# Decay attention and a two-layer MLP on one core: the first batch's decay made on GpSimd, its rows turned in float32, the weights converted by block

## The chip, the cores and the metric

The kernel runs on one core of one Trainium2 chip. The metric is device time in microseconds (us) for one execution. The engines are TensorE (PE, with its weight loads shown apart as PEld), VectorE (DVE), ScalarE (ACT), GpSimd (POOL) and SyncE (SP), which here only issues transfers. Each engine runs its own instructions in the order in which they stand. Transfers are issued on SP's queue, on POOL's queue and, for the output, on ACT's queue, and run on 16 DMA engines.

## The reference, cut to what matters

```python
# q, k, v: 8 batches x 8 heads x 576 rows x 64;  f: 8 x 8 x 576
scores = q @ k.T / sqrt(64)
cum    = cumsum(log(clip(f, 1e-4, 1)))            # per head, along the rows
scores = where(causal, -1e9, scores + cum[:, None] - cum[None, :])
attn   = exp(scores - max) / (sum + 1e-9)
x      = concat over heads (attn @ v)             # 4608 tokens x 512
h      = x @ w_in                                 # w_in 512 x 2048, stored as float64
g      = where(h >= 1, h, where(h <= -1, 0, (h + 1)**2 / 4))
out    = g @ w_out                                # w_out 2048 x 512, stored as float64
```

## The kernel before, in words

**Attention** is cut into 36 jobs, each one pair of heads of one batch. The first batch is cut once more along the query rows (`CUTS`): jobs 0 to 3 are its four pairs with rows 0 to 255, jobs 4 to 7 the same pairs with rows 256 to 575; from job 8 on, four jobs make a batch. A job goes by blocks of 128 query rows (r = 0 to 4, the last with 64 rows and both heads in one tile).

A job's steps are: q and k are loaded (`load`, line 400) and turned (`prepare`; jobs below `NQK` = 12 keep them in float32, later ones split them in two float16 parts and turn these by a DMA transpose, `qkT<-qs`). `scores` multiplies them (line 511). The decay, cum of the row minus cum of the column, enters in one of two ways. For jobs below `NDEC` = 8, that is the whole first batch, six bfloat16 rows per head (`w.dec`, loaded from `dec_d` at line 416 into a buffer of the ring `vm`) are multiplied into the same PSUM tile, and the causal mask comes from the constant tiles `hide`. From job 8 on, a row of cum is broadcast to 128 partitions (`ck`, line 411, POOL's queue) and POOL makes decay (line 521) and mask (line 525) in an SBUF tile `sdr` or `sd`. `weights` then adds score and decay on DVE and takes the row minimum of the negated sum (line 604), ACT does the exponential (line 608). For jobs below `NPE` = 5 `turn_rows` multiplies the weights by a diagonal matrix on PE in float32, which scales and transposes them at once (lines 545 and 551), ACT copies them to `pT` (line 556), and `early_values` multiplies by v in float32 (line 576). From job 5 on the rows are split into two float16 parts (ACT line 622, DVE line 628, or POOL line 626 for some of jobs 6 and 7), turned by DMA transposes (`pT<-pr`, lines 634 and 637), and multiplied by v in three float16 passes (`values`, line 648). The result goes to `x` (ACT line 583 or 657, DVE line 584 or 658).

**Scales.** From batch 1 on `value_scale` takes the largest |v| of a batch, and from batch 2 on `query_scale` the largest |q| and |k|. Each reads its arrays in tiles of 288 KB on POOL's queue (lines 282 and 306) into `vm`, a ring of two buffers, and takes a maximum on DVE (lines 283 and 307). A load waits until a buffer of `vm` is free. `across` makes a maximum common to all partitions: a transpose on PE (line 125), four small DVE operations, a product on PE (line 135) between them, and `scale_of` three more on DVE.

**Weights.** They come as 32 pieces of 512 KB (float64). Each is packed to float32 by three DVE operations (lines 232, 235, 238), then scaled into a high and a low float16 part: ACT line 259; POOL lines 261 and 262 for w_in, DVE line 264 for w_out. `weight_split` handles half a block (two pieces): the bound for the scale is a maximum on DVE for w_in (line 248) and a sum of |w| on ACT for w_out (line 252), then one `across` per half block, 16 in all. `CONVERT` and `LOADS` tell in which job; `RAW` tells where a raw piece waits.

**The MLP** goes by units: 256 tokens times one of 8 blocks of d_ff, 144 units. `moe_front` (line 690) and `moe_back` (line 718) are PE's, with ACT and DVE between them (lines 699 to 704). A unit can run when its tokens are in `x` and its block is converted; `quota` spreads the ready units over the jobs. `EARLY` lets units of the first 256 tokens begin with the blocks that are converted.

The program is written in this order, and a scheduler then sets the order on each engine and each queue ahead of the run.

Of the kernel before, what the change touches and what calls it, by code (L numbers as in the profile page):

```python
# [10 lines left out]
BF16 = mybir.dt.bfloat16  # L11
# [5 lines left out]
P = 128  # L17
# [12 lines left out]
NPE = 5  # L30

NQK = 12
NDEC = 8

POOL_LOW = {6: (2, 4), 7: (2, 4)}
# [3 lines left out]
CONVERT = {3: 3, 4: 3, 5: 4, 6: 4, 7: 2}  # L39
LOADS = {0: 2, 1: 3, 2: 4}  # L40
AHEAD = 4

RAW = (
    (1, 2), (3, 4), (5, 6), (7, 8), (9, 10), (11, 12), (16, 17), (18, 19),
    (20, 13), (14, 15), (11, 12), (16, 17), (18, 19), (20, 14), (15, 16), (17, 18),
# [4 lines left out]
def kernel(  # L50
# [10 lines left out]


# [80 lines left out]
    NR = 6  # L143
    NDH = NDEC // (2 * NPAIR) * H
    dec_d = dram.tile([NDH, NR, 2, S], BF16, name="dec_d")
# [3 lines left out]
    def decay_sums():  # L149

# [3 lines left out]
        rows = one.tile([P, NT5, 2, 2, S], F16, name="pT").rearrange("p t l h s -> p (t l h s)").bitcast(BF16)  # L154
        rows = rows[0:NDH, 0:NR * 2 * S].rearrange("p (r j s) -> p r j s", r=NR, j=2)
        nc.gpsimd.memset(fl[0:nb, 3 * S:4 * S], 0.0)
        nc.gpsimd.memset(rows[:, 1::2, 0], 1.0)
        nc.gpsimd.memset(rows[:, 0::2, 1], 1.0)
# [3 lines left out]
        nc.scalar.activation(fl[0:nb, S:2 * S], fl[0:nb, 0:S], AF.Ln)  # L162
        cum = fl[0:nb, 2 * S:3 * S]
# [3 lines left out]
        rest = fl[0:NDH, 0:S]  # L167
        nc.vector.tensor_scalar(out=rest, in0=cum[0:NDH], scalar1=8.0, scalar2=None, op0=ALU.mult)
        for i in range(3):
            part = rows[:, 2 * i, 0]  # L170
            nc.scalar.activation(part, rest, AF.Copy)
            nc.scalar.activation(rows[:, 2 * i + 1, 1], part, AF.Copy, scale=-1.0)
            if i < 2:
                nc.vector.tensor_tensor(out=rest, in0=rest, in1=part, op=ALU.subtract)
# [3 lines left out]
        twice = fl[0:nb, S:S + P]  # L178
# [12 lines left out]
    hides = one.tile([P, 2, 2, SP], F16, name="qs").rearrange("p j l e -> p (j l e)").bitcast(F32)  # L191
    hide, hide4 = hides[:, 0:FULL], hides[:, FULL:FULL + S]
    for t, h in ((hide, 1), (hide4, 2)):
        n = P // h
        wide = t.shape[1]
        nc.gpsimd.memset(t, 0.0)
        for i in range(h):
            a = t[n * i:n * i + n, wide - n:wide]
            nc.gpsimd.affine_select(
                a, a, pattern=[[-1, n]], channel_multiplier=1, base=0, compare_op=ALU.is_ge, fill=MASKED  # L200
            )


# [9 lines left out]
    def weight_load(n):  # L213
        i, j = divmod(n, 2)
        if j == 0:
            src = w_in.bitcast(I32)[:, i * 4 * P:(i + 1) * 4 * P].rearrange("(t p) c -> p t c", p=P)
        else:
            src = w_out.bitcast(I32)[i * 2 * P:(i + 1) * 2 * P, :].rearrange("(t p) c -> p t c", p=P)
        n = src.shape[1] // 2
        for k_, slot in enumerate(RAW[2 * i + j]):  # L220
            nc.sync.dma_start(
                slots[slot].rearrange("p (t c) -> p t c", t=n), src[:, n * k_:n * (k_ + 1), :]
            )

    def weight_split(n):
        i, j = divmod(n, 2)
        parts = []
        for k_, slot in enumerate(RAW[n]):
# [12 lines left out]
            parts.append((top.bitcast(F32), slice(k_ * DM, (k_ + 1) * DM)))  # L241
        hi = place[n][:, 0]
        lo = place[n][:, 1]
        m1 = tiny.tile([P, 1], F32, name="m1", bufs=2)
        ms = tiny.tile([P, 2], F32, name="ms", bufs=2)
        for k_, (wf, c) in enumerate(parts):
            if j == 0:
                nc.vector.tensor_reduce(
                    out=ms[:, k_:k_ + 1], in_=wf, axis=AX.X, op=ALU.max, apply_absolute_value=True
                )  # L250
# [7 lines left out]
        for wf, c in parts:  # L258
            nc.scalar.activation(hi[:, c], wf, AF.Copy, scale=s)
            if n % 2 == 0:  # L260
                nc.gpsimd.tensor_scalar(out=wf, in0=wf, scalar1=s, scalar2=0.0, op0=ALU.mult, op1=ALU.add)
                nc.gpsimd.tensor_tensor(out=lo[:, c], in0=wf, in1=hi[:, c], op=ALU.subtract)
            else:
                nc.vector.scalar_tensor_tensor(
                    out=lo[:, c], in0=wf, scalar=s, in1=hi[:, c], op0=ALU.mult, op1=ALU.subtract
                )
# [219 lines left out]
    def scores(w, r):  # L486
# [28 lines left out]
        if w.p < NDEC:  # L515
            return
# [360 lines left out]
```

## Time and profile before

| | |
|---|---|
| time, median of 3 runs | 1243.08 us (1237.45 to 1243.55) |
| the profiled execution | 1248.13 us; its span, first to last instruction, 1246.4 us |
| PE busy | 1071.5 us, 86% of the span |
| DVE, ACT, POOL busy | 830.1 us, 765.8 us, 438.7 us |
| mean granted TensorE clock | 0.930 |
| DMA | 163.27 MB, mean 131 GB/s |

Busy shares are means over the whole span. The profile also gives the span in 40 slices, tables of the engines' busy time in any stretch, and rows of single instructions with the idle time before them and what ended it. The table's "PEclk" is the clock that was granted to TensorE as a share of full speed.

### The profile page before, as it was taken

The numbers are of one execution on the slowest core, as the hardware profiler recorded it, in microseconds if no ns is written. First come the engines' busy times: TensorE is split into PE (matmuls) and PEld (weight loads), VectorE is DVE, ScalarE is ACT, GpSimd is POOL, SyncE is SP. The second block draws the span as 40 slices with busy tenths as digits, with TensorE's granted clock in tenths as the row PEclk, the third lists the DMA queues.
The fourth block names the chain that finished last, engine by engine and source line by source line (L and its number), as shares of the span: only waits on it lengthen the run. The fifth ranks groups of instructions, "written<-read, shape, count | busy, mean of one in ns | idle before, by whom it ended". The sixth has DMA issues, their size and how long they took to land. (4 is left out here: it accounts for less than half of the span.)

```text
span 1246.4 us, 24524 instructions
## 1 busy us (share of the span) xinstructions
PE 1071.5 (86%) x8859; PEld 675.2 (54%) x8859; DVE 830.1 (67%) x2227; ACT 765.8 (61%) x1564; POOL 438.7 (35%) x752
## 2 busy tenths in 40 slices
PE   1569646798327988999999999999999999999998
PEld 1336333454215654665666666656566566667665
DVE  5747879788658777877765576687766877622222
ACT  2456545466436586777766676686777777734443
POOL 2021244464455463544532323454534444100000
PEclk9868767699667998999999999999999999999999
DMA  8822564598999888886756656577777675500000
GB/s 235 277 51 63 143 151 147 143 205 205 180 206 210 179 171 155 163 162 137 147 104 110 127 111 114 120 141 151 141 135 141 128 130 90 93 17 3 18 18 17
DMA packets 404906, 163.27 MB, mean 131 GB/s; under 512 B 384840, under 2 KB 384840, under 8 KB 404776
## 3 DMA queue, kind: packets, MB, share of 16 engines
q1 hardware_dynamic: 389040, 113.33, 48.6%
q0 software_dynamic: 10560, 38.94, 11.6%
q10 hardware_dynamic: 5184, 9.44, 2.1%
q8 instruction: 69, 1.13, 0.4%
q14 instruction: 53, 0.43, 0.1%
HBM read 86.61 MB, written 9.70 MB: 77 GB/s over the span
## 5 line engine op out<-in xcount | busy, mean ns | idle before, releaser
L690 PE MATMUL ph<-x,place 128*128 128x256 f16 (+3 forms) x4608 | 436.1, 249 | 36.9 <-DVE u L701 23.9
L718 PE MATMUL po<-place,g 128*128 128x512 f16 x1728 | 415.9, 383 | 7.1 <-ACT g L703 4.8
L690 PEld LDWEIGHTS <-place 128*128 128x128 f16 x4608 | 355.2, 99 | 115.7 <-issue 41.1
L718 PEld LDWEIGHTS <-g 128*128 128x128 f16 x1728 | 162.3, 99 | 181.3 <-issue 9.5
L521 POOL TENSOR_SCALAR sdr<-ck,nsig,cqs 128x128 f32<-128x128 f32 (+1 forms) x192 | 156.7, 820 | 290.4 <-DVE pr L628 278.0
L608 ACT ACTIVATE sdr<-sdr,nm 128x384 f32<-128x384 f32 (+1 forms) x248 | 137.8, 557 | 117.4 <-DVE nm L604 116.7
L701 DVE SCALAR_TENSOR_TENSOR u<-ph,z,u 128x512 f32<-128x512 f32 x136 | 101.5, 747 | 106.2 <-ACT u L700 105.8
L699 ACT ACTIVATE u<-ph,z 128x512 f32<-128x512 f32 x136 | 104.5, 768 | 76.3 <-PE ph L690 75.4
L628 DVE SCALAR_TENSOR_TENSOR pr<-sdr,rc,pr 128x384 f16<-128x384 f32 (+2 forms) x232 | 122.0, 561 | 38.9 <-ACT pr L622 36.2
L703 ACT ACTIVATE g<-u,z 128x512 f16<-128x512 f32 x136 | 97.7, 719 | 74.0 <-DVE u L701 73.5
L622 ACT ACTIVATE pr<-sdr,rc 128x384 f16<-128x384 f32 (+1 forms) x236 | 119.8, 556 | 34.2 <-ACT sdr L608 14.1
L704 DVE SCALAR_TENSOR_TENSOR g<-u,z,g 128x512 f16<-128x512 f32 x136 | 104.2, 766 | 47.6 <-ACT g L703 47.4
L648 PE MATMUL big<-pT,vs 128*64 128x64 f16 (+3 forms) x1098 | 94.7, 300 | 34.7 <-DMA pT<-pr 33.2
L604 DVE CUSTOM_DVE_ANT_0 sdr<-s,sdr,nalpha 128x128 f32<-128x128 f32 (+1 forms) x192 | 98.5, 546 | 21.3 <-PE s L511 13.1
L511 PE MATMUL s<-qkT 64*128 64x128 f16 (+5 forms) x704 | 91.7, 356 | 20.2 <-DVE nm L604 16.0
L648 PEld LDWEIGHTS <-vs 128*64 128x64 f16 x1098 | 61.5, 117 | 74.5 <-issue 45.6
L700 ACT ACTIVATE u<-u 128x512 f32<-128x512 f32 x144 | 89.7, 624 | 2.4
L525 POOL TENSOR_SCALAR_AFFINE_SELECT sdr<-sdr 128x128 f32<-128x128 f32 x224 | 77.4, 352 | 7.7
L521 POOL TENSOR_SCALAR sd<-ck,nsig,cqs 64x576 f32<-64x576 f32 x48 | 46.1, 960 | 78.2 <-DMA ck<-cum_d 65.5
L511 PEld LDWEIGHTS <-qkT 64*128 64x128 f16 (+1 forms) x864 | 33.2, 99 | 58.2 <-issue 44.6
L433 DVE SCALAR_TENSOR_TENSOR qs<-qk,sqk,qs 128x640 f16<-128x640 f32 x48 | 42.3, 907 | 27.3 <-ACT qs L432 26.9
L432 ACT ACTIVATE qs<-qk,sqk 128x640 f16<-128x640 f32 x48 | 37.1, 819 | 36.2 <-DMA qkT<-qs 30.3
(174 smaller groups left out, 1077.8 us busy)
## 6 DMA issues: line engine op xcount, KB each, us to landing
ck<-cum_d POOLq DMA_DIRECT2D x56, 288.0 KB, 4.7
out_dram<-ot ACTq DMA_DIRECT2D x36, 256.0 KB
qk<-in_k_dram SPq DMA_DIRECT2D x64, 128.0 KB
vm<-in_v_dram POOLq DMA_DIRECT2D x28, 288.0 KB, 3.9
v<-in_v_dram SPq DMA_DIRECT2D x62, 128.0 KB
qk<-in_q_dram SPq DMA_DIRECT2D x56, 128.0 KB
vm<-in_q_dram POOLq DMA_DIRECT2D x24, 288.0 KB, 3.5
vm<-in_k_dram POOLq DMA_DIRECT2D x24, 288.0 KB, 3.8
```

The source lines that it names most:

```text
L511: nc.tensor.matmul(outs[h][:, c0:c1], lhsT=x[rows], rhs=y[rows, c0:c1], start=(i == 0), stop=(i == len(terms) - 1),)
L521: nc.gpsimd.tensor_scalar(out=sd[p0:p1, 0:wid], in0=w.ck[h][p0:p1, 0:wid], scalar1=w.nsig if w.p < NQK else w.nsig[p0:p1], scalar2=w.cqs[p ...
L604: nc.vector.tensor_tensor_reduce(out=a, in0=sp, in1=other, scale=w.nalpha, scalar=BIG, op0=ALU.add, op1=ALU.min, accum_out=nm[:, i:i + 1],)
L608: nc.scalar.activation(a, a, AF.Exp, bias=nm[:, i:i + 1], scale=-1.0, accum_out=sm[:, i:i + 1])
L622: nc.scalar.activation(pr[:, :, 0, i, :], a, AF.Copy, scale=rc[:, i:i + 1])
L628: nc.vector.scalar_tensor_tensor(out=pr[:, :, 1, i, :], in0=a, scalar=rc[:, i:i + 1], in1=pr[:, :, 0, i, :], op0=ALU.mult, op1=ALU.subtract,)
L648: nc.tensor.matmul(av[64 * h:64 * h + 64, at + s0:at + s1], lhsT=w.vs[:, vl, h, t, :], rhs=w.pT[:, t, pl, h, s0:s1], start=(t == 0 and pi ...
L690: nc.tensor.matmul(ph[:, fi, a0:a1], lhsT=wi[fb][:, wl, t, fi * P:(fi + 1) * P], rhs=xs[b][:, t, xl, s0:s0 + a1 - a0], start=(fi == 0 and ...
L699: nc.scalar.activation(u, h, AF.Relu, scale=z.u[:, i:i + 1], bias=z.h[:, i:i + 1])
L701: nc.vector.scalar_tensor_tensor(out=u, in0=h, scalar=z.t[:, i:i + 1], in1=u, op0=ALU.max, op1=ALU.min)
L704: nc.vector.scalar_tensor_tensor(out=g[:, 1], in0=u, scalar=z.r[:, i:i + 1], in1=g[:, 0], op0=ALU.mult, op1=ALU.subtract)
L718: nc.tensor.matmul(po[ch][i], lhsT=g[:, gl, fi * TC + i * P:fi * TC + (i + 1) * P], rhs=wo[fb][:, wl, fi, :], start=(first and fi == 0 and ...
```

## The change

- **Decay.** `NDEC` and all that belongs to it go: the six bfloat16 rows, `dec_d`, their loads on SP, the product of six rows, the `hide` tiles. Jobs 0 to 7 take the way of the later jobs: `ck`, and decay and mask on POOL. For jobs below 12 the load of `ck` moves from POOL's queue to SP's, and only the columns in use are loaded. The ring `vm` no longer holds decay rows.
- **Weights.** `weight_split` handles a whole block, four pieces; both bounds are sums of |w| on ACT, and one `across` takes two columns: 8 in place of 16. `CONVERT`, `LOADS`, `AHEAD` and `RAW` are new: conversion runs from job 1 to job 6 (before, 3 to 7).
- **Rows of the first batch.** `NPE` goes from 5 to 8: jobs 5, 6 and 7 use `turn_rows` and `early_values`. `POOL_LOW` goes.

```diff
-NPE = 5
+NPE = 8
...
-NDEC = 8
-
-POOL_LOW = {6: (2, 4), 7: (2, 4)}
...
-CONVERT = {3: 3, 4: 3, 5: 4, 6: 4, 7: 2}
-LOADS = {0: 2, 1: 3, 2: 4}
-AHEAD = 4
+CONVERT = {1: 1, 2: 1, 3: 1, 4: 2, 5: 2, 6: 1}
+LOADS = {0: 2, 1: 3}
+AHEAD = 3
...
-        nc.sync.dma_start(dec_d, rows)
         nc.sync.dma_start(cum_d, cum)
...
-        for k_, (wf, c) in enumerate(parts):
-            if j == 0:
-                nc.vector.tensor_reduce(
-                    out=ms[:, k_:k_ + 1], in_=wf, axis=AX.X, op=ALU.max, apply_absolute_value=True
-                )
+            if k_ < 0:
+                nc.vector.tensor_reduce(out=m, in_=wf, axis=AX.X, op=ALU.max, apply_absolute_value=True)
             else:
-                nc.scalar.activation(lo[:, c], wf, AF.Abs, accum_out=ms[:, k_:k_ + 1])
+                nc.scalar.activation(low.bitcast(F32), wf, AF.Abs, accum_out=m)
+        m1 = tiny.tile([P, 2], F32, name="m1w", bufs=2)
         nc.vector.tensor_reduce(out=m1, in_=ms, axis=AX.X, op=ALU.max)
-        m = mi[:, i:i + 1] if j == 0 else tiny.tile([P, 1], F32, name="m2")
+        m = tiny.tile([P, 2], F32, name="m2", bufs=2)
         across(m, m1)
-        s = sw[:, j, i:i + 1]
-        scale_of(s, mp[:, j, i:i + 1], m)
+        nc.vector.tensor_copy(mi[:, i:i + 1], m[:, 0:1])
+        scale_of(sw[:, :, i], mp[:, :, i], m)
...
-        if w.p >= NDEC:
-            ck = two.tile([P, S], F32, name="ck", bufs=3)
-            nc.gpsimd.dma_start(ck, cum_d[bh:bh + 1].broadcast_to([P, S]))
-            w.ck.append(ck)
-            return
-        if h == 0:
-            w.dec = two.tile([P, S], F32, name="vm").bitcast(BF16).rearrange("p (j s) -> p j s", j=2)
-        nc.sync.dma_start(w.dec[64 * h:64 * h + NR], dec_d[bh])
+        ck = two.tile([P, S], F32, name="ck", bufs=3)
+        (nc.sync if w.p < NQK else nc.gpsimd).dma_start(ck[:, 0:w.s1], cum_d[bh:bh + 1, 0:w.s1].broadcast_to([P, w.s1]))
+        w.ck.append(ck)
...
-        if w.p < NDEC:
-            terms.append((w.dec[:, 0, s0 + w.s0:s1 + w.s0], w.dec[:, 1], NR))
...
-        if w.p < NDEC:
-            return
...
-            other = a if w.p >= NDEC else hide[:, FULL - wid:FULL] if r < LAST else hide4
```

What moves in the order of the instructions stands in three places. In the changed kernel line numbers are smaller: 185 for 221, 372 for 411 and 416, 244 and 268 for 282 and 306, 245 and 269 for 283 and 307, 474 and 478 for 521 and 525, 556 for 604.

SP's queue near the start, before: `place` and `in_moe` are weight pieces, `vm<-dec_d` the decay rows of jobs 0 and 1.

```order
L221 DMA place_108<-in_moe_w_in_dram 128x2x512
L221 DMA place_109<-in_moe_w_in_dram 128x2x512
L400 DMA qk_0_132<-in_q_dram 128x2x64 x2
L404 DMA qk_0_132<-in_q_dram 64x2x64
L404 DMA qk_0_132<-in_k_dram 64x2x64
L221 DMA place_110<-in_moe_w_out_dram 128x1024
L221 DMA place_111<-in_moe_w_out_dram 128x1024
L404 DMA qk_1_133<-in_q_dram 64x2x64
L404 DMA qk_1_133<-in_k_dram 64x2x64
L416 DMA vm<-dec_d 6x1152 x4
```

The same queue now:

```order
L362 DMA qk_0_119<-in_q_dram 128x2x64 x2
L362 DMA qk_0_119<-in_k_dram 128x2x64 x2
L185 DMA place_100<-in_moe_w_in_dram 128x2x512
L372 DMA ck<-cum_d 128x256 x3
L185 DMA place_101<-in_moe_w_in_dram 128x2x512
L185 DMA place_102<-in_moe_w_out_dram 128x1024
```

The first job's decay stands behind one weight piece, where eight stood ahead of it.

POOL's queue near the start, now (before, three loads of `ck` and the low parts of the weights stand here, and no line 521 or 525 until job 8):

```order
L244 DMA vm<-in_v_dram 128x576 x2
L268 DMA vm<-in_q_dram 128x576
L474 TENSOR_SCALAR sdr_122<-ck,cq_89 128x128
L474 TENSOR_SCALAR sdr_124<-ck,cq_89 128x256
L474 TENSOR_SCALAR sdr_123<-ck,cq_89 128x128
L478 AFFINE_SELECT sdr_122<-sdr_122 128x128
L474 TENSOR_SCALAR sdr_125<-ck,cq_89 128x256
L474 TENSOR_SCALAR pr_132<-ck,cq_89 128x128
L474 TENSOR_SCALAR pr_134<-ck,cq_89 128x256
L268 DMA vm<-in_q_dram 128x576
L478 AFFINE_SELECT sdr_124<-sdr_124 128x128
```

Loads of later batches' q, k and v now stand among the decay of the first jobs; each waits on POOL for a buffer of `vm`.

DVE in job 9, before:

```order
L307 TENSOR_REDUCE m_5298<-vm 128x1
L115 RECIPROCAL sqk<-mk 128x2
L316 TENSOR_SCALAR nsig<-sqk 128x1
L319 RECIPROCAL nalpha<-nsig 128x1
L320 TENSOR_SCALAR cqs_129<-cq_90,nsig 128x40
L433 SCALAR_TENSOR_TENSOR qs<-qk_0_132,sqk,qs 128x640 x2
L604 ISA sdr_135,nm<-s,sdr_135 128x384
```

DVE in job 6, now, among the packing of weight pieces:

```order
L228 SCALAR_TENSOR_TENSOR place_103<-place_104,sw,place_103 128x512
L269 TENSOR_REDUCE m_5265<-vm 128x1 x3
L196 TENSOR_SCALAR u<-place_106 128x512
L269 TENSOR_REDUCE m_5265<-vm 128x1
L199 SCALAR_TENSOR_TENSOR u<-place_106,u 128x512
L648 SCALAR_TENSOR_TENSOR u<-ph,early_z,u 128x512
L202 SCALAR_TENSOR_TENSOR place_106<-place_106,u 128x512
```

The same maxima stand three jobs earlier. Counted over DVE's order: ahead of job 7's write to `x` stand 21 of them before and 56 now, ahead of job 11's 65 and 68. On PE, ahead of job 7's product with v stand the fronts of 8.4 units before and 6.0 now, ahead of job 11's 16.9 and 16.5, and ahead of job 35's 113.6 and 114.8.

More of the change, by code (lines that the diff above doesn't have):

```diff
@@ L10 @@
 F16 = mybir.dt.float16
-BF16 = mybir.dt.bfloat16
 I32 = mybir.dt.int32
@@ L166, in decay_sums @@
         )
[L167 to L174, printed above, removed]
-        nc.sync.dma_start(dec_d, rows)
         nc.sync.dma_start(cum_d, cum)
         pt = ps1.tile([P, 1024], F32, name="big")
-        twice = fl[0:nb, S:S + P]
+        twice = fl[0:nb, 0:P]
         nc.vector.tensor_copy(
@@ L240, in weight_split @@
             )
[L241 to L245, printed above, removed]
-        for k_, (wf, c) in enumerate(parts):
-            if j == 0:
-                nc.vector.tensor_reduce(
-                    out=ms[:, k_:k_ + 1], in_=wf, axis=AX.X, op=ALU.max, apply_absolute_value=True
-                )
-            else:
-                nc.scalar.activation(lo[:, c], wf, AF.Abs, accum_out=ms[:, k_:k_ + 1])
+            wf = top.bitcast(F32)
@@ L255, in weight_split @@
         across(m, m1)
-        s = sw[:, j, i:i + 1]
-        scale_of(s, mp[:, j, i:i + 1], m)
-        for wf, c in parts:
-            nc.scalar.activation(hi[:, c], wf, AF.Copy, scale=s)
-            if n % 2 == 0:
+        nc.vector.tensor_copy(mi[:, i:i + 1], m[:, 0:1])
+        scale_of(sw[:, :, i], mp[:, :, i], m)
+        for k_, wf in enumerate(wfs):
+            j = k_ // 2
+            s = sw[:, j, i:i + 1]
+            c = slice(k_ % 2 * DM, (k_ % 2 + 1) * DM)
+            hi, lo = place[2 * i + j][:, 0, c], place[2 * i + j][:, 1, c]
+            nc.scalar.activation(hi, wf, AF.Copy, scale=s)
+            if k_ < 2:
@@ L763, in load_weights @@
         nonlocal nload
-        while nload < min(n, 2 * NB) and not any(set(RAW[nload]) & set(r) for r in RAW[nw:nload]):
+        while nload < min(n, NB) and not any(set(RAW[nload]) & set(r) for r in RAW[nw:nload]):
             weight_load(nload)
@@ L837 @@
             while ready() and done - before < quota * (i + 1) // len(steps):
-                if units[done] not in bsc and nw < 2 * NB:
+                if units[done] not in bsc and nw < NB:
                     break
```

79 lines of the change are left out of this document (29 added, 50 removed).

## The prediction

> **What bounds the kernel now.** I read the page's shares and slices first, then the table of engines by stretch, then the rows that bound the stretches.
>
> ```profile
> PE 1071.5 (86%) x8859; PEld 675.2 (54%) x8859; DVE 830.1 (67%) x2227; ACT 765.8 (61%) x1564; POOL 438.7 (35%) x752
> ...
> PE   1569646798327988999999999999999999999998
> ...
> PEclk9868767699667998999999999999999999999999
> DMA  8822564598999888886756656577777675500000
> ```
>
> The mean of 86% hides two halves: from slice 13 on PE is full, ahead of it are holes, a lower granted clock and, in slices 9 to 13, full DMA engines. The ends of the stretches come from ACT's rows that write `x`: job 7 (last of batch 0) and job 11 (last of batch 1).
>
> ```profile
> 238.44 0.44 ACT L657 ACTIVATE x<-big 128x320 f16<-128x320 f32 x1 [8.90 <-PE big L648]
> ...
> 380.00 0.65 ACT L657 ACTIVATE x<-big 128x576 f16<-128x576 f32 x1 [1.65 <-PE big L648]
> ```
>
> ```profile
> core 0: us, PE busy (x) PEld busy (x) DVE busy (x) ACT busy (x) POOL busy (x), PEclk, DMA share, GB/s
> 0.00:238.00 238.00, 145.22 (x767) 85.48 (x767) 170.02 (x504) 115.96 (x254) 64.75 (x96) 0.77 0.56 153
> 238.00:380.00 142.00, 91.87 (x627) 52.45 (x629) 104.25 (x301) 73.56 (x167) 70.67 (x131) 0.83 0.90 193
> 380.00:600.00 220.00, 200.12 (x1904) 129.20 (x1902) 171.14 (x473) 157.81 (x332) 111.68 (x191) 0.96 0.86 165
> 600.00:1246.00 646.00, 634.27 (x5565) 408.08 (x5564) 384.65 (x951) 418.46 (x813) 191.63 (x335) 1.00 0.51 97
> ```
>
> After 600 us PE is busy 634 of 646 us, and by the counts in the part on the change as many units are left after job 11 as before (16.9 fronts done, then 16.5). So the end moves with job 11's end, less what the stretch 380 to 600 (20 us of PE idle) gives or takes; I set that at zero. The sum has two parts: **stretch one**, 0 to 238, and **stretch two**, 238 to 380.
>
> **Stretch two.** Its fullest resource is DMA: 0.90 of 142 is 128 us.
>
> ```profile
> q1 hardware_dynamic: 47152, 11.70, 49.4%
> q0 software_dynamic: 3940, 14.54, 37.8%
> ...
> vm<-in_k_dram POOLq DMA_DIRECT2D x16, 288.0 KB, 4.0
> vm<-in_q_dram POOLq DMA_DIRECT2D x13, 288.0 KB, 3.4
> vm<-in_v_dram POOLq DMA_DIRECT2D x13, 288.0 KB, 4.0
> ck<-cum_d POOLq DMA_DIRECT2D x8, 288.0 KB, 5.1
> ```
>
> POOL's queue q0 carried 50 loads in 37.8% of 142, 53.7 us, so 1.07 us of all 16 engines for each. Of the maxima for which `vm` is loaded, 44 stand between job 7's and job 11's writes (21 to 65); now 12 (56 to 68). The ring is free from the start, since decay rows no longer sit in it, and the scheduler has drawn the loads into batch 0. DMA loses 32 x 1.07 = 34 us and comes to 94. DVE loses the maxima:
>
> ```profile
> L307 DVE TENSOR_REDUCE m<-vm 128x1 f32<-128x576 f32 x48 | 35.7, 747 | 23.4 <-DMA vm<-in_k_dram 12.7 <-DMA vm<-in_q_dram 10.0
> ...
> L248 DVE TENSOR_REDUCE ms<-place 128x1 f32<-128x512 f32 x12 | 8.0, 677 | 0.1
> ...
> L127 DVE TENSOR_REDUCE top<-s 1x1 f32<-1x128 f32 x24 | 6.5, 273 | 5.3 <-PE s L125 5.2
> ...
> L136 DVE COPY m<-s 128x1 f32<-128x1 f32 x8 | 1.2, 154 | 7.2 <-PE s L135 7.2
> ```
>
> 32 x 0.747 = 24 us, so 104 becomes 80. PE gets more: 10.5 fronts stand in the stretch (6.0 to 16.5) where 8.5 stood (8.4 to 16.9).
>
> ```profile
> L690 PE MATMUL ph<-x,place 128*128 128x256 f16 (+3 forms) x4608 | 436.1, 249 | 36.9 <-DVE u L701 23.9
> L718 PE MATMUL po<-place,g 128*128 128x512 f16 x1728 | 415.9, 383 | 7.1 <-ACT g L703 4.8
> ```
>
> A unit is (436.1 + 415.9) / 144 = 5.9 us, two are 12 (14 at this stretch's clock of 0.83), so PE comes to 104 and is now the fullest. Before, the fullest filled 0.90 of the stretch; PE at the same share needs 104 / 0.90 = 115 us. **Gain 26 us**, between 0 (the jobs' own chains set the pace, whatever the DMA does) and 38 (PE full).
>
> That chains and DMA, not PE, set the pace there shows in its last two jobs, and what chains alone do in jobs 3 and 4:
>
> ```profile
> 52.00:79.00 27.00, 19.52 (x100) 12.16 (x98) 9.50 (x40) 13.23 (x39) 2.00 (x3) 0.68 0.47 114
> 79.00:109.00 30.00, 21.72 (x102) 14.29 (x102) 17.97 (x74) 20.93 (x50) 7.46 (x9) 0.60 0.13 30
> ...
> 317.00:351.00 34.00, 13.97 (x84) 6.73 (x83) 18.41 (x52) 15.71 (x39) 16.26 (x34) 0.63 1.06 196
> 351.00:380.00 29.00, 9.00 (x73) 5.54 (x74) 19.15 (x62) 10.10 (x25) 12.70 (x22) 0.65 0.98 205
> ```
>
> **Stretch one, term by term.** DVE is busy 170 of 238 us; 29.5 of its 68 idle us lie between 52 and 109, where conversion (from job 3 on) had not begun.
>
> Opening. The first product waits for the decay rows behind eight weight pieces on SP:
>
> ```profile
> 20.26 0.80 PE L511 MATMUL s<-qkT 64*128 64x128 f32 x4 [0.25 <-DVE mv L136]
> 35.59 0.47 PE L511 MATMUL s<-vm 6*128 6x128 bf16 x2 [14.52 <-DMA vm<-dec_d]
> ```
>
> Now `ck` stands behind one piece. At best 14.5 us go; DVE packed weights meanwhile, and must still pack them. I take -8, about half; bounds -14.5 and 0.
>
> Conversion. 16 maxima leave DVE: 16 x 0.677 = 10.8 us. Eight of 16 rounds of `across` and `scale_of` go, each eight small operations, of which the rows show 0.154 and 0.273 us: 8 x 8 = 64 of them, 10 to 17 us, and their waits for PE, (5.3 + 7.2) us in these rows. Where DVE is nearly full this lies on the path, where it idles not. I take -15 for work and -5 for waits; bounds -33 and 0. The sums on ACT that replace the maxima are behind ACT's 122 idle us; with that cover gone 16 more sums of about a maximum's length, 11 us.
>
> Maxima moved in. 35 (21 to 56) x 0.747 = 26 us on DVE, and the waits of DVE and POOL for their loads as stretch two shows them over 42 loads:
>
> ```profile
>   DVE m L307: 22.2, 7
>   DVE rc L619: 10.1, 5
>   DMA vm<-in_v_dram: 9.2, 5
>   DMA vm<-in_k_dram: 8.9, 4
> ...
>   DMA vm<-in_q_dram: 6.4, 3
> ```
>
> DVE waited 24.5 us in 42 loads, 0.58 each, so 20 for 35. Part fills the 29.5 idle us. I take +10 for work of 0 to 26, and +8 for waits of 0 to 20. DMA at 0.56 has room for 37 us more.
>
> Decay on POOL. Jobs 0 to 3 have two row blocks, 4 to 7 three, two heads each: 40 additions and 40 masks.
>
> ```profile
> L521 POOL TENSOR_SCALAR sd<-ck,cq 64x576 f32<-64x576 f32 x8 | 7.2, 904 | 6.3 <-DMA ck<-cum_d 5.8
> ...
> L521 POOL TENSOR_SCALAR sdr<-ck,cq 128x128 f32<-128x128 f32 x8 | 4.5, 567 | 2.6 <-DVE pr L628 2.0
> ```
>
> At 0.567 to 0.904, masks bounded by the same rows from above and nothing from below, 23 to 72 us; I take 42, under the middle since a mask touches 128 columns alone, for POOL's 173 idle us. It is hidden as long as POOL runs a block ahead of DVE; the mask comes into the chain at the opening, where I take +4; bounds 0 and 42. If that cover is gone, the score row, ACT's exponential and the row's turn wait behind it.
>
> Float32 turn in jobs 5 to 7. Job 4 does it already, at 21.7 us of PE and 0.13 of DMA in 30 us (79 to 109); the changed jobs replace a wait on transposes by a wait on PE and ACT. I take 0, between -9 (the 8.90 us that job 7's write waited) and +23 (PE's 21.72 there less the 13.97 of job 10, whose rows go by transposes, three times). The products of six rows go, under 0.5 us each at the 0.47 shown; inside the opening's term.
>
> Loads of `ck`. Sixteen are new in batch 0, and those of jobs 8 to 11 move from POOL's queue to SP's, behind weight pieces and the loads of q, k and v; twelve transposes leave SP. On DMA the sixteen are at most 16 x 1.07 = 17 us, on top of the 37, in 105 idle us. I take 0, since they stand a job ahead of their use; one that comes late by its whole landing time costs the POOL chain 5.1 us, so 16 x 5.1 = 82 us if all did, and nothing in the rows makes all late.
>
> Stretch one: -8 - 15 - 5 + 10 + 8 + 4 = **-6 us**. Both stretches: -32. On the profiled execution's 1248.1 us that is 1216; the median of the runs shown is 5 us lower, so **1211 us**.
>
> **The rivals.**
>
> *Given back in batch 0.* The moved maxima and waits go in at full price, +46 in place of +18: stretch one +22, stretch two -26, in all -4, 1239 us. For it: DVE is the busiest engine from 109 to 238 and the loads only change place. Against: 29.5 us of idle DVE.
>
> *POOL's queue stalls batch 0 (slower).* In the opening four `vm` loads wait for buffers ahead of the first decay; POOL waited 22.2 + 10.1 us in the two rows above alone for 42 loads, so 27 for 35. If that and the 42 us of decay come whole between score and exponential, the forecast's -32 loses its +4 for decay and takes +69: +33, 1276 us. It makes the kernel slower as soon as 36 of the 69 us are on the path; at 35 it is 1242. Against: POOL is idle 173 of 238 us, and DVE has weights to pack while it waits, as in the opening above.
>
> *POOL holds DVE up.* Rows of the profile show it:
>
> ```profile
> 220.12 4.26 DVE L342 TENSOR_SCALAR early_z<-early_z 128x2 int32<-128x2 int32 x1
> ...
> L238 DVE SCALAR_TENSOR_TENSOR place<-place,u x9: 660/682/1897, 118.5 to 194.5; 128x512 int32<-128x512 int32 x9
> ```
>
> An operation on two columns took 4.26 us, a packing step up to 1.9. If each added us on POOL held DVE, 42 in place of the 4: +6, 1249 us. With one packing step in nine held by 1.2 us, the 64 two-input steps cost 8 us: 1219. The Trainium skill ("SBUF — State Buffer", "Who interferes with whom") says that DVE operations with two SBUF inputs and GpSimd operations that read SBUF exclude each other for a whole instruction. By that rule, these rows agree, the added decay is paid for by DVE and this rival decides.
>
> *More than that.* Opening, conversion and waits at their bounds (-47 +10 +8 +4 = -25), stretch two at PE's bound (-38): -63, 1180 us. For it: DVE, ACT and DMA all have room in both stretches then. Against: DVE is nearly full from 109 us on, and in-order engines have not filled a stretch before 600 us yet.
>
> **How the numbers follow.** Chances: the forecast 0.57, given back 0.15, POOL's queue 0.09, POOL against DVE 0.05, more 0.14. The forecast's own range is 1190 to 1230; to leave out no more than 2 in 10 I go to 1180, which the last rival reaches, and 1242, which holds the first. A change under 0.5%, 6 us, is about what cannot be told from none. Faster: the forecast, the last rival and a part of the first, 0.76; same 0.13, the rest of that case; slower 0.11, POOL's queue and the worse half of POOL against DVE.
>
> **What would show it.** Right: job 11's `x` near 348 us (job 7's near 232), some 12 loads of `vm` between them, DMA well under 0.90 and PE near it there, no wait over 5 us for the first decay. Wrong: job 7's `x` after 245 us with DVE waiting for POOL (queue) or DVE rows of over 1 us beside POOL's (port); job 11's `x` early and the end not, with new PE idle after 380; or stretch two still at 35 us a job with DMA no longer full, which would mean that chains set it.

## The result, and the profile after

The changed kernel takes **1198.1 us**, the median of 4 runs (1195.69 to 1200.78); the kernel before took 1242.91 beside it (1237.45 to 1243.55). The ratio is 0.9649, with a 95% interval of 0.9615 to 0.9684: some 44 us faster. The forecast was 1211, in a range of 1180 to 1242. Medians and ratios below are of executions in the faster of two states that a program can fall into; one kernel, `before + conversion`, had a slow one among its four, which is the profiled one, so its profile is left out of the table.

The page of the changed kernel, shares and slices:

```profile
PE 1064.8 (89%) x8871; PEld 681.6 (57%) x8871; DVE 806.8 (68%) x2140; ACT 770.4 (65%) x1599; POOL 476.1 (40%) x811
...
PE   2566766998689899999999999999999999999998
...
PEclk9767888999789999999999999999999999999999
DMA  8797744689989977867665555777767773300000
```

TensorE's work is nearly the same, 1064.8 us where it was 1071.5. What went is its idle time: the span less the busy time was 1246.4 - 1071.5 = 174.9 us and is 1193.9 - 1064.8 = 129.1. PE is at eight tenths or more from slice 11 on, counted from 0; before it was so from slice 13 on.

ACT's rows that write `x` at the end of job 7 and of job 11 (line 536 now, and 604), and the table of engines by stretch, cut at these ends:

```profile
222.18 0.51 ACT L536 ACTIVATE x<-big,sv 128x320 f16<-128x320 f32 x1
...
328.98 0.65 ACT L604 ACTIVATE x<-big 128x576 f16<-128x576 f32 x1
```

```profile
core 0: us, PE busy (x) PEld busy (x) DVE busy (x) ACT busy (x) POOL busy (x), PEclk, DMA share, GB/s
0.00:222.00 222.00, 136.20 (x737) 88.61 (x738) 172.91 (x498) 123.24 (x301) 129.68 (x203) 0.82 0.71 211
222.00:329.00 107.00, 92.10 (x671) 54.61 (x670) 81.35 (x233) 72.15 (x158) 46.84 (x88) 0.92 0.86 168
329.00:549.00 220.00, 202.97 (x1919) 130.30 (x1917) 168.16 (x466) 158.25 (x336) 107.00 (x186) 0.97 0.81 160
549.00:1193.00 644.00, 633.49 (x5551) 408.06 (x5549) 384.37 (x946) 416.76 (x808) 192.62 (x335) 1.00 0.51 97
```

Stretch one went from 238.4 to 222.2 us (-16), stretch two from 141.6 to 106.8 (-35), and from job 11's end on nothing is lost: 866.4 us to the end before, 864.9 now. In stretch one POOL's busy time has doubled, from 64.75 to 129.68 us. In stretch two DMA and DVE did just what the forecast set for them: 0.86 x 107 = 92 us of DMA (94 forecast) and 81 us of DVE (80). PE needed 92 us there, not 104: its granted clock was 0.92, not the 0.83 of before.

### The profile page after: what moved, and what is told of

Same layout as the page of the kernel before. It is cut to its first block, busy times and chain, and to the rows that moved or that the text cites. A ratio compares the mean times of both kernels' runs of the same rounds, so it can differ in the third digit from the quotient of the medians.

```text
span 1193.9 us, 24608 instructions
## 1 busy us (share of the span) xinstructions
PE 1064.8 (89%) x8871; PEld 681.6 (57%) x8871; DVE 806.8 (68%) x2140; ACT 770.4 (65%) x1599; POOL 476.1 (40%) x811
## 5 line engine op out<-in xcount | busy, mean ns | idle before, releaser
L637 PE MATMUL ph<-x,place 128*128 128x256 f16 (+3 forms) x4608 | 430.3, 248 | 10.1 <-DVE u L648 8.0
L474 POOL TENSOR_SCALAR sdr<-ck,nsig,cqs 128x128 f32<-128x128 f32 (+1 forms) x192 | 154.3, 808 | 297.7 <-DVE pr L575 278.5
L560 ACT ACTIVATE sdr<-sdr,nm 128x128 f32<-128x128 f32 (+1 forms) x240 | 132.6, 553 | 75.8 <-DVE nm L556 75.1
L575 DVE SCALAR_TENSOR_TENSOR pr<-sdr,rc,pr 128x128 f16<-128x128 f32 (+1 forms) x224 | 116.3, 555 | 39.9 <-ACT pr L574 37.7
L574 ACT ACTIVATE pr<-sdr,rc 128x128 f16<-128x128 f32 (+1 forms) x224 | 112.6, 550 | 18.9 <-ACT sdr L560 14.3
L466 PE MATMUL s<-qkT 64*128 64x128 f16 (+5 forms) x704 | 88.3, 347 | 26.7 <-DVE nm L556 23.9
L595 PE MATMUL big<-pT,vs 128*64 128x64 f16 (+3 forms) x1008 | 83.8, 291 | 18.6 <-DMA pT<-pr 10.8
L478 POOL TENSOR_SCALAR_AFFINE_SELECT sdr<-sdr 128x128 f32<-128x128 f32 x240 | 85.0, 363 | 7.8
L595 PEld LDWEIGHTS <-vs 128*64 128x64 f16 x1008 | 53.1, 113 | 51.6 <-issue 33.2
```

Of the source, the lines that this page charges most:

```text
L466: nc.tensor.matmul(outs[h][:, c0:c1], lhsT=x[rows], rhs=y[rows, c0:c1], start=(i == 0), stop=(i == len(terms) - 1),)
L474: nc.gpsimd.tensor_scalar(out=sd[p0:p1, 0:wid], in0=w.ck[h][p0:p1, 0:wid], scalar1=w.nsig if w.p < NQK else w.nsig[p0:p1], scalar2=w.cqs[p ...
L560: nc.scalar.activation(a, a, AF.Exp, bias=nm[:, i:i + 1], scale=-1.0, accum_out=sm[:, i:i + 1])
L574: nc.scalar.activation(pr[:, :, 0, i, :], a, AF.Copy, scale=rc[:, i:i + 1])
L575: nc.vector.scalar_tensor_tensor(out=pr[:, :, 1, i, :], in0=a, scalar=rc[:, i:i + 1], in1=pr[:, :, 0, i, :], op0=ALU.mult, op1=ALU.subtract,)
L595: nc.tensor.matmul(av[64 * h:64 * h + 64, at + s0:at + s1], lhsT=w.vs[:, vl, h, t, :], rhs=w.pT[:, t, pl, h, s0:s1], start=(t == 0 and pi ...
```

## The experiments

Every kernel ran in at least three rounds against the kernel before on the same chip; over the groups of runs its median was 1241.5 to 1243.7, so times are compared as they are. "Job n" is the time at which that job's first write to `x` starts, in the profiled execution; "PE idle" is the span less PE's busy time. All in us.

| kernel | median | ratio, 95% interval | job 0 | job 7 | job 11 | job 13 | span | PE idle |
|---|---|---|---|---|---|---|---|---|
| before | 1242.9 | 1 | 51.6 | 238.4 | 380.0 | 449.5 | 1246.4 | 174.9 |
| changed | 1198.1 | 0.9649 (0.9615 to 0.9684) | 39.9 | 222.2 | 329.0 | 388.8 | 1193.9 | 129.1 |
| before, ring free | 1229.3 | 0.9896 (0.9855 to 0.9936) | 54.2 | 235.0 | 359.1 | 416.5 | 1226.8 | 156.2 |
| changed, ring held | 1200.5 | 0.9667 (0.9625 to 0.9708) | 32.9 | 210.2 | 335.3 | 394.0 | 1196.8 | 133.6 |
| before + conversion | 1211.8 | 0.9762 (0.9671 to 0.9853) | | | | | | |
| before + turn | 1239.0 | 0.9981 (0.9940 to 1.0022) | 51.4 | 222.0 | 363.8 | 431.1 | 1236.3 | 145.1 |
| before + decay on POOL | 1252.2 | 1.0075 (1.0041 to 1.0108) | 36.9 | 241.8 | 371.8 | 440.0 | 1251.1 | 178.3 |
| changed, old conversion | 1227.0 | 0.9878 (0.9821 to 0.9935) | 36.8 | 221.4 | 360.8 | 418.1 | 1225.9 | 143.7 |
| changed, old turn | 1217.2 | 0.9792 (0.9751 to 0.9834) | 39.5 | 226.4 | 333.6 | 401.3 | 1211.8 | 156.2 |
| changed, decay on PE | 1219.4 | 0.9823 (0.9757 to 0.9889) | 58.9 | 238.3 | 351.5 | 410.7 | 1219.5 | 136.8 |
| changed, POOL's decay twice | 1218.2 | 0.9804 (0.9770 to 0.9839) | 44.8 | 240.1 | 350.1 | 409.5 | 1221.0 | 144.0 |
| changed, low parts on DVE | 1209.2 | 0.9744 (0.9703 to 0.9785) | 40.9 | 227.5 | 338.8 | 397.9 | 1206.9 | 134.0 |
| changed, two more turned | 1201.1 | 0.9696 (0.9632 to 0.9759) | 38.7 | 222.2 | 325.7 | 388.1 | 1200.2 | 117.3 |
| changed, short ring of rows | 1204.4 | 0.9681 (0.9639 to 0.9723) | 38.6 | 218.7 | 328.7 | 386.5 | 1202.2 | 133.0 |

### Is it the ring `vm`?

Stretch two was forecast from 32 loads and maxima that move ahead of it because the ring is free. Two runs, one edit each: the ring freed in the kernel before,

```diff
-            w.dec = two.tile([P, S], F32, name="vm").bitcast(BF16).rearrange("p (j s) -> p j s", j=2)
+            w.dec = two.tile([P, S], F32, name="ck", bufs=3).bitcast(BF16).rearrange("p (j s) -> p j s", j=2)
```

> The kernel before, with one edit: the decay rows of batch 0 lie in the buffers of ck, which nobody uses before job 8, so the ring vm is free from the start. By the order of DVE 38 of the maxima stand ahead of job 7's write (before 17 loads of vm, in the changed kernel 52). Theory (the loads drawn ahead into batch 0 are the gain of stretch two): 21 of the 35 moved loads, so 21/35 of the 35 us that stretch two lost, some 20 us: 1223 us, with stretch two near 120 us. Rival (the float32 turn and the conversion make the gain, the ring does nothing): 1240 us or more, stretch two near 140.

and the ring held in the changed one, by one row of `ck` for each job of the first batch.

```diff
-        ck = two.tile([P, S], F32, name="ck", bufs=3)
+        if w.p < 8 and h == 0:
+            ck = two.tile([P, S], F32, name="vm")
+        else:
+            ck = two.tile([P, S], F32, name="ck", bufs=3)
```

> The changed kernel, with one edit: for jobs 0 to 7 the row of cum for head 0 lies in the ring vm, so that the ring is held in batch 0 as before. 36 loads of vm stand ahead of job 7's write in place of 52, 60 ahead of job 9's in both. Theory: 16 loads go back to stretch two, 16 us of DMA and 12 of DVE there, less what stretch one gains: 1205 to 1213 us. Rival (the ring does nothing): 1198 us.

Freed alone, the ring takes the time from 1242.9 to 1229.3 us, 14 us: 38 loads of `vm` stand ahead of job 7 in the order, 17 before. That is nearer to the theory's 1223 than to the rival's 1240, and stretch two took 124 us (120 expected). Held in the changed kernel (36 loads ahead of job 7 for 52), it shortens stretch one by 12 us, lengthens stretch two by 18, and at 1200.5 us the time is within the interval of the changed kernel's: the rival's time. So the 16 loads cost 12 us in stretch one or 18 in stretch two, about 1 us each **wherever they stand**, and of the 6 us that separate the two kernels at job 11 only 2 are left at the end. The loads did leave stretch two, as forecast, but in the changed kernel moving them is not what made it faster. That loads only change place is the mechanism of the prediction's rival "Given back in batch 0", though its time did not come.

### The three parts, apart and together

Conversion undone in the changed kernel, and alone in the kernel before (the old, or the new, `weight_load`, `weight_split`, `CONVERT`, `LOADS`, `AHEAD` and `RAW`, as in the diff of the change):

> The changed kernel with the weights converted by half blocks as before (maxima on DVE for w_in, 16 rounds of across, conversion in jobs 3 to 7). Theory: conversion is worth the -20 us of the sum, 1213 to 1220 us, all of it in stretch one. Rival (it lies beside other work): 1198 to 1203.

> The kernel before with the conversion by block alone. Theory: -20 us, 1223. Rival: the same 1243, since the ring vm is still held and batch 0 still ends with DMA transposes.

Measured: 1227.0 with it undone, 7 us beyond the theory, and 1211.8 with it alone (1216.2 over all four executions, the figure that a later expectation uses), where the theory had 1223.

The turn undone, and alone:

```diff
-NPE = 8
+NPE = 5
```

> The changed kernel with NPE = 5: jobs 5 to 7 split their rows in two float16 parts and turn them by DMA transposes again, all on DVE (no part on POOL). Theory (that step is worth 0, between -9 and +23): 1198 to 1208 us, since DVE gets 9 low parts of 0.6 to 0.9 us and three of v back. Rival (the transposes taken off DMA in batch 0 are the gain): 1215 us or more, with job 7's end late by 15 us.

> The kernel before with the float32 turn for jobs 5 to 7 alone. By the sum it is worth 0: 1243. By the run that undid it in the changed kernel, 19 us: 1224.

Measured: 1217.2 with it undone, the rival's time, though job 7 ends only 4 us later and not 15; and 1239.0 with it alone, nearer to what the sum says.

The decay back on PE, with its six rows held in the ring `ck` so that `vm` stays free, and the decay on POOL alone, which is the old conversion and `NPE = 5` together in the changed kernel (six low parts of jobs 6 and 7 that POOL made in the kernel before are DVE's then, as in the change):

> The changed kernel with the decay of jobs 0 to 7 back on PE (six bfloat16 rows, as before), these rows in the buffers of ck so that vm stays free; conversion by block and the float32 turn as changed. Theory now, after doubling POOL's additions cost 20 us for 28: POOL's 42 us of decay cost the changed kernel some 25 to 30 us of stretch one, so 1170 to 1175 us, job 7's end before 205. Rival (the first copy of the decay is hidden, only a second one is not): 1195 us or more.

> The kernel before with the decay on GpSimd for all jobs alone (weights by half block and five jobs turned in float32, as before; the two steps of the rows' low part that GpSimd did for jobs 6 and 7 are on VectorE as in the change); nothing is left out. The other two parts alone gave 1216 (conversion) and 1239 us (turn), and decay with turn 1227. Theory (the decay on GpSimd is worth its opening and the free vm buffers, and costs GpSimd time in jobs 1 to 4): job 0's x is written near 40 us in place of 51.6, job 7 between 228 and 238, the end 1222 to 1235 us. Rival (only with the other parts is it worth anything, since VectorE has the old conversion to do meanwhile): within 5 us of 1243.

Both theories failed. With the decay on PE the changed kernel takes 1219.4 us, where the theory saw it faster than the changed one; that lies in the rival's range. With the decay on POOL alone the kernel before takes 1252.2, more than either side set, although job 0 ends at 36.9 us as the theory had it.

Read as squares (of two parts: neither, one, the other, both), the ratios say this. **Conversion** is worth 2.4% alone, and 2.3% where the other two parts are there (0.9878 to 0.9649): 29 us both times, though alone with 11 us of uncertainty to each side. **Decay and turn** are worth 1.2% together without the conversion (0.9878) and 1.1% with it (0.9762 to 0.9649, uncertain by 1.0% to each side), some 14 us, and neither alone is worth anything: the turn -0.2%, inside its interval, and the decay on POOL is *slower* by 0.75%, although it frees the ring, worth 14 us by itself. Set beside the ring alone, POOL's decay costs 1252.2 - 1229.3 = 23 us there. With the conversion in it is the same: the decay alone added gives 0.9792 and the turn alone, with the ring free, 0.9823, neither below the 0.9762 of the conversion by itself.

Where conversion's 29 us lie is seen with the old one back. Job 7 ends at the same time (221.4 and 222.2); then job 8 takes 58.9 us in place of 22.1. The table by stretch of that kernel, for job 8 and job 11:

```profile
221.40:280.30 58.90, 52.32 (x354) 32.03 (x351) 47.58 (x147) 32.29 (x70) 23.75 (x46) 0.94 0.65 154
...
339.90:360.80 20.90, 9.14 (x77) 5.09 (x79) 16.27 (x63) 10.64 (x26) 10.65 (x19) 0.67 1.07 213
```

In the order of that kernel, eight units (fronts 6.0 to 14.0) fall into job 8, which they fill, and 0.3 are left for job 11, where PE is busy 9 of 21 us while DMA is full. In the changed kernel job 8 has three units and job 9 five. Jobs 9 and 10 together take 59.6 us with 2.5 units under the old conversion, and 60.9 us with 7.3 in the changed kernel: the 4.8 units more, 28 us of PE at the 5.9 us for each that the prediction worked out, cost next to no time there. Earlier conversion spreads the units over jobs that wait for DMA. No run moved the units by themselves.

What decay on POOL brings is the opening. With the decay on PE (and the new loads of weights) the first product waits for the decay rows, row of PE:

```profile
41.87 0.46 PE L509 MATMUL s<-ck 6*128 6x128 bf16 x2 [22.81 <-DMA ck<-dec_d]
```

Job 0 ends at 58.9 us there and at 39.9 in the changed kernel: 19 us, of which 16 are still there at job 7, and the distance is 22.5 us at job 11 and in the end 21. Part of the 19 is place on the queue: in the kernel before the same product waited 14.52 us, at 35.59. No run had the decay on PE with its rows loaded ahead of the weight pieces, so how much of this POOL itself brings is not shown.

### Is POOL's work hidden?

Forty decay additions more, the same value written a second time:

```diff
-            nc.gpsimd.tensor_scalar(
+            for _ in range(2 if w.p < 8 else 1):
+                nc.gpsimd.tensor_scalar(
```

> The changed kernel with each of POOL's 40 decay additions of jobs 0 to 7 made twice (the second writes the same again): 28 us more of POOL in stretch one, all of it reading and writing SBUF. Theory (POOL's decay is hidden but for some 4 us in 42): 1198 to 1204 us. Rivals (POOL's work holds DVE up, by its port or by its queue): up to 28 us more, 1215 to 1226 us.

POOL's groups of instructions ahead of job 7 in the changed kernel (additions, line 474; masks, line 478), the same additions when issued twice (each with 11 additions of jobs 8 and 9 among them), and the table by stretch of the kernel that issues them twice:

```profile
L474 POOL TENSOR_SCALAR sdr<-ck,cq 128x128 f32<-128x128 f32 (+3 forms) x24 | 21.7, 902 | 12.1 <-DMA ck<-cum_d 6.6 <-PE ph L498 3.8
...
L474 POOL TENSOR_SCALAR pr<-ck,cq 128x128 f32<-128x128 f32 (+4 forms) x18 | 13.6, 754 | 2.2 <-DMA ck<-cum_d 0.5
...
L478 POOL TENSOR_SCALAR_AFFINE_SELECT sdr<-sdr 128x128 f32<-128x128 f32 x24 | 10.3, 450 | 0.4
...
L474 POOL TENSOR_SCALAR sd<-ck,cq 64x576 f32<-64x576 f32 x9 | 8.8, 974 | 6.1 <-DMA ck<-cum_d 4.8 <-ACT g L650 0.6
...
L478 POOL TENSOR_SCALAR_AFFINE_SELECT pr<-pr 128x128 f32<-128x128 f32 (+1 forms) x18 | 6.3, 363 | 0.5
...
L478 POOL TENSOR_SCALAR_AFFINE_SELECT sd<-sd 64x64 f32<-64x64 f32 x9 | 2.8, 310 | 0.6
```

```profile
L475 POOL TENSOR_SCALAR pr<-ck,cq 128x128 f32<-128x128 f32 (+4 forms) x36 | 29.2, 810 | 4.9 <-PE ph L499 1.4 <-ACT pr L561 0.3
L475 POOL TENSOR_SCALAR sdr<-ck,cq 128x128 f32<-128x128 f32 (+3 forms) x40 | 27.8, 694 | 7.8 <-DMA ck<-cum_d 2.8 <-ACT qkT L409 1.3 <-DMA vm<-in_q_dram 0.3
L475 POOL TENSOR_SCALAR sd<-ck,cq 64x576 f32<-64x576 f32 x15 | 13.3, 885 | 7.2 <-DMA ck<-cum_d 4.1 <-PE ph L505 1.9
```

```profile
0.00:240.10 240.10, 145.19 (x738) 92.11 (x739) 177.54 (x498) 124.05 (x302) 151.68 (x243) 0.85 0.66 193
```

The additions took 44.1 us and take 70.3: 26 more, of which 20 reach the time (1218.2 against 1198.1) and 18 job 7's end. They are not hidden, though POOL is idle 88 of 240 us. DVE is busy only 4.6 us longer, 3.9 of them in one line's operations on at most two columns (line 563); its 64 packing steps with two inputs take 46 us in both kernels, and took 47 before. DVE waits 12.0 us for POOL's additions and masks where it waited 4.9, and 12.6 us for weight pieces where it waited 4.5.

POOL's decay is crowded into the first part of the stretch, where it has little idle time to hide in: the last addition of the first batch starts at 133.0 us, though DVE takes up that row only at 197.9. The table by stretch of the changed kernel, cut at the ends of jobs 0, 3 and 4:

```profile
0.00:39.90 39.90, 13.43 (x54) 8.26 (x54) 25.75 (x63) 15.66 (x41) 13.89 (x36) 1.00 0.85 261
39.90:88.80 48.90, 27.92 (x121) 18.14 (x123) 38.45 (x123) 30.95 (x86) 38.82 (x53) 0.62 0.88 262
88.80:112.80 24.00, 15.85 (x82) 11.45 (x84) 22.76 (x61) 16.40 (x44) 20.41 (x27) 0.72 0.69 192
```

POOL is busy 59 of 73 us in jobs 1 to 4, 81%, where the mean over the stretch was 58%. If that were all, work taken from POOL would come back as time. So w_in's low parts went to DVE, one operation there for two on POOL:

```diff
-            if k_ < 2:
+            if k_ < 0:
```

> The changed kernel, with the low parts of w_in made by one two-input operation on VectorE in place of two operations on GpSimd; nothing is left out. Theory (GpSimd is on the path of the first batch: 28 us more on it cost 20 us of time in the run that issued the decay twice): about 30 us leave GpSimd's 130 us ahead of job 7's end and some 12 us come to VectorE, so job 7's x is written 5 to 15 us earlier than at 222 us and the time is 1184 to 1194 us. Rival (VectorE, busy 173 of 222 us, sets the batch): its 12 us come on top, job 7 at 225 to 234 us, 1201 to 1210 us.

```profile
0.00:222.00 222.00, 136.00 (x682) 87.36 (x683) 170.24 (x510) 121.64 (x295) 88.22 (x164) 0.78 0.71 208
```

POOL lost 41 us, and jobs 3 and 4 end 1.5 and 1.9 us earlier; then jobs 5 and 6 end at 150.3 and 191.0 us (144.5 and 181.9), and the time is 11 us longer. The rival's time came, 1201 to 1210, and job 7 at 227.5 is in its range too. POOL is not the bound by its sum: work moved from it to DVE gains nothing. What it is worth to lift work from POOL without giving it to DVE was not run. That added work costs so much because it stands in the chain ahead of the scores of the first jobs, and that DVE is the other engine in the way, fits both runs but is argued, not shown; DVE's busy time up to 222 us is no longer than in the changed kernel.

### Why decay and turn need each other

A job that is turned by DMA has score rows for two blocks in flight; one that is turned in float32 has four (`more`, line 483 of the kernel before). POOL writes the decay into these rows, so it can run further ahead. Waits of POOL in jobs 5 to 7 (us in all, times, longest), with decay on POOL alone:

```profile
POOL sdr L476 <- DVE pr L577: 12.7, 3, 6.5
```

In the changed kernel:

```profile
POOL sdr L474 <- PE ph L498: 1.6, 2, 1.2
```

That made a theory; the test keeps the turn and takes the extra rows away.

```diff
-            ring = sdr + more if w.p < NPE else sdr
+            ring = sdr + more if w.p < 5 else sdr
...
-            ring = sd4 + [prs[LAST]] if w.p < NPE else sd4
+            ring = sd4 + [prs[LAST]] if w.p < 5 else sd4
```

> The changed kernel, jobs 5 to 7 still turned in float32, but with the shorter ring of score rows that jobs turned by DMA have (two row blocks in flight in place of four); nothing is left out. GpSimd writes the decay into that ring. Theory (decay and float32 turn gain only together, since the turn lends GpSimd the four more buffers and it can run two blocks ahead): in jobs 5 to 7 GpSimd waits for rows to be freed, 5 us or more in all where the changed kernel has 2, job 7's x is written 4 to 12 us after 222 us, and most of the 19 us that the undone turn cost come back: 1207 to 1220 us. Rival (it is the transposes and VectorE's low parts that the turn saves, and the ring is no matter): job 7 at 219 to 225 us, 1194 to 1203 us.

```profile
POOL sdr L474 <- PE ph L498: 3.8, 2, 2.7
POOL sdr L474 <- ACT sdr L560: 1.9, 1, 1.9
POOL sdr L474 <- DVE pr L575: 1.1, 1, 1.1
```

Measured: 1204.4 us. The waits came, 6.8 us of them (in the last row POOL already waits for a row of a later job, which is split on DVE), but job 7 did *not* end later (218.7 against 222.2), close to the rival's 219 to 225; the time lies between the two sides. It is 6 us longer than the changed kernel's, with intervals that overlap, and the order then has 2.3 units less done by job 13 (21.6 fronts against 23.9), which is where the table by stretch shows the loss. From 329 to 400 us, in the changed kernel, with the old turn and with the short ring:

```profile
329.00:400.00 71.00, 63.51 (x656) 42.44 (x653) 57.25 (x150) 51.65 (x112) 39.17 (x73) 0.95 0.86 177
```

```profile
329.00:400.00 71.00, 53.70 (x529) 36.39 (x531) 50.18 (x145) 42.44 (x95) 34.74 (x64) 0.85 0.94 164
```

```profile
329.00:400.00 71.00, 54.34 (x587) 36.64 (x585) 52.24 (x129) 42.85 (x93) 36.88 (x63) 0.88 0.90 169
```

PE is idle 7.5, 17.3 and 16.7 us there. Part of what an edit to jobs 5 to 7 costs thus arrives in jobs 12 and 13, where the scheduler has placed other units. The theory that the rows explain the pair falls for the most part: 6 of the 19 us at best. A rival that no run tests is left: the six low parts of jobs 6 and 7 go to DVE when the decay alone is on POOL, and are gone when the rows are turned in float32 as well; POOL's 12.7 us of waits above are for DVE's low parts. What makes decay and turn worth more together stays open.

### More of the same

If the turn pays by taking transposes from DMA, it should pay in jobs 10 and 11 too.

```diff
+TURN = (0, 1, 2, 3, 4, 5, 6, 7, 10, 11)
...
-        if w.p < NPE:
+        if w.p in TURN:
```

> The changed kernel with jobs 10 and 11, the last two of the second batch, turned in float32 on TensorE too in place of DMA transposes; nothing is left out. Units are set a little later in the order (14.0 fronts done ahead of job 11's end in place of 16.8). Theory (what the float32 turn is worth is DMA time taken from a stretch in which TensorE has room: there DMA is at 0.92 and 1.02 of its time and TensorE busy 20 of 22.5 and 14 of 23.8 us): jobs 10 and 11 end 5 to 10 us earlier for 2.8 units less, worth 16 us, done by then, so the end is 1190 to 1204 us, no worse than the changed kernel by more than 6. Rival (TensorE's work is what counts from job 8 on): the turns' 7 us of TensorE for each job are added, 1205 to 1215 us.

Measured: 1201.1 us, in the theory's range but no difference that can be told from the changed kernel. Jobs 10 and 11 end 4.2 and 3.3 us earlier, less than expected. PE's idle time falls by 12 us, and its busy time rises by 18 (1082.9 us).

## Why the prediction was right, and where not

**Right: the sign, the two stretches, and that nothing changes after them.** Both ends came earlier than forecast, at 222 us (232) and 329 (348). The case "more than that", with -25 and -38, set -63 against the -52 of the profiled executions; the forecast had -32. That the sum came this near is in part luck: its -6 for stretch one holds -20 for a part that, undone, leaves the end of job 7 where it is, and its -26 for stretch two was put down to loads that, moved back, cost 2 us in the end.

**Stretch two, -35 for -26.** The step that failed is the size of PE's share: two units at "14 at this stretch's clock of 0.83", PE 104 us, the fullest, at 0.90 (104 is the sum with 12 for the two units; with its 14 it is 106). The clock was 0.92 and PE came to 92 us, at 0.86 of a shorter stretch. DMA's 94 and DVE's 80 held. The cause was given too narrowly: the loads left, but holding the ring changed the time by 2.4 us. With 36 loads ahead of job 7 the stretch is 125 us if the ring is held, and 139 us, with 37, under the old conversion: the spread of the units over jobs 8 to 11, which the forecast counted (10.5 fronts) but did not place, is what conversion by block brings.

**Opening, -12 for -8.** Job 0 ends 11.7 us earlier, four fifths of the bound of 14.5. Rows of the changed kernel:

```profile
22.42 1.61 POOL L474 TENSOR_SCALAR sdr<-ck,cq 128x128 f32<-128x128 f32 x3 [3.34 <-DMA ck<-cum_d]
24.09 0.29 POOL L478 TENSOR_SCALAR_AFFINE_SELECT sdr<-sdr 128x128 f32<-128x128 f32 x1
...
24.42 0.29 DVE L556 CUSTOM_DVE_ANT_0 sdr<-s,sdr 128x128 f32<-128x128 f32 x1 [1.62 <-POOL sdr L478]
24.49 0.48 POOL L474 TENSOR_SCALAR sdr<-ck,cq 128x256 f32<-128x256 f32 x1
```

No wait over 5 us for the first decay, as set; DVE waits 1.62 us for the mask.

**Decay on POOL, +4 of 42.** The forty additions and forty masks of the first batch took 36.3 + 16.4 = 52.8 us (the groups above, 44.1 + 19.4, hold 11 of each for later jobs), inside 23 to 72, and "for POOL's 173 idle us" was the wrong reading: a mean over 238 us, where the condition stood in the same paragraph ("as long as POOL runs a block ahead"). Without the turn the decay is slower; with it, the next 26 us cost 20. The rival "POOL's queue stalls batch 0" had the sign of the kernel with this part alone; that its mechanism is the queue was not shown. "POOL holds DVE up" is there, but no larger than before: DVE's operations on at most eight columns that took over 0.7 us, held as the last section shows, come to 6.8 us in stretch one and came to 6.5.

**Maxima moved in, +18.** They are there, 52 loads ahead of job 7 after 17 (four maxima more read another buffer). Who waited for `vm` in stretch one of the changed kernel (us, times):

```profile
  POOL vm L268: 20.8, 10
  POOL vm L244: 16.3, 7
  DVE m L269: 8.4, 9
  DVE m L245: 4.9, 8
```

DVE waits 13.3 us for 52 loads, 0.26 each, where 0.58 was set. POOL waits 37 us for DVE to free buffers, 0.71 for each load, about as set in the rival (27 for 35). With the ring held, 16 loads fewer are worth 12 us of stretch one, 0.75 each, so for 35 the two terms come to 26, not 18.

**Float32 turn, 0.** Right by itself (-4 us, not to be told from none), wrong in company: undone, it costs 19 us. No term of the sum could show that, since each was priced as if it stood alone.

**Conversion, -20.** Put in stretch one as DVE's work and waits; it is worth 29 us, and with the old one job 7 ends no later.

## What to carry to other kernels

A part's price depends on what the other parts have filled: here one part was slower alone (+9 us) and two were worth 14 us only together, so a change of several parts is measured as a square of kernels, not as a sum. Idle time that is to hide work is read in the jobs where the work falls, not as a mean over the stretch. Ask where the *units* that fill waiting jobs come to lie: an edit that leaves its own jobs untouched can lose its time two batches on.

## What the runs showed of the hardware that was not expected

A decay addition of 128 x 256 took 0.48 us at the opening (row above). Later two additions, one of 128 x 128 and one of 128 x 256, took 6.30 us together, the second 5.29, while DVE packed weights beside them. The shortest, the median and the longest of the two in ns, and rows of POOL and DVE at that time, in the changed kernel:

```profile
L474 POOL TENSOR_SCALAR sdr<-ck,cq x2: 917/3102/5286, 46.4 to 47.5; 128x128 f32<-128x128 f32 x1, 128x256 f32<-128x256 f32 x1
```

```profile
46.45 6.30 POOL L474 TENSOR_SCALAR sdr<-ck,cq 128x128 f32<-128x128 f32 x2 [1.18 <-DMA ck<-cum_d]
46.53 0.68 DVE L199 SCALAR_TENSOR_TENSOR u<-x,u 128x512 int32<-128x512 int32 x1
...
48.47 0.66 DVE L199 SCALAR_TENSOR_TENSOR u<-place,u 128x512 int32<-128x512 int32 x1
...
51.80 0.67 DVE L199 SCALAR_TENSOR_TENSOR u<-place,u 128x512 int32<-128x512 int32 x1
```

DVE's steps with two inputs kept 0.66 to 0.68 us all the while; six of them ran from start to end beside the long addition. The forecast had named this as a rival with DVE as the one that pays; the rows show POOL paying, and POOL's queue with it. The Trainium skill ("SBUF — State Buffer", "Who interferes with whom") says that a DVE instruction with two SBUF inputs contends with a GpSimd instruction that reads SBUF, and that the port pair that they share is an exclusive lock. These rows fit that, with DVE in possession through several instructions in a row; no run took DVE's steps away, so that it is the cause was not shown.

The opposite happens too. Small DVE operations with a single tensor input, which mostly take 0.15 to 0.25 us, were held while POOL made low parts of w_in (line 226, two inputs). Two cases of the changed kernel:

```profile
128.67 2.65 DVE L308 TENSOR_SCALAR early_z<-early_z 128x3 f32<-128x3 f32 x1
...
129.01 1.17 POOL L226 TENSOR_TENSOR place<-place,place 128x512 f16<-128x512 f32 x1
130.13 1.15 POOL L226 TENSOR_TENSOR place<-x,place 128x512 f16<-128x512 f32 x1
```

```profile
155.77 1.41 DVE L563 TENSOR_SCALAR rc<-sm 128x2 f32<-128x2 f32 x1
...
155.99 1.16 POOL L226 TENSOR_TENSOR place<-place,place 128x512 f16<-128x512 f32 x1
```

All four such operations over 0.7 us in stretch one (on at most eight columns, the longest 2.65) end 0.02 to 0.04 us after a line 226 does. The prediction's row of 4.26 us in the kernel before, also of one tensor input, ends in the same way 0.03 us after POOL's line 262. In the kernel with the low parts on DVE, where POOL has no such operation, none takes over 0.7 us up to the end of job 7. So what holds them that long here is POOL's two-input step, and not the decay.
